# One transfer for a set of query or key rows, with the token order restored later, in a bucketed-attention and maxout kernel

## The chip, the cores and the metric

The kernel runs on one core of one Trainium2 chip. The metric is the device time of one execution in microseconds (us); the median of several runs is compared. Five engines work side by side, each on its own queue of instructions and in order: TensorE (PE; PEld is its weight load), VectorE (DVE), ScalarE (ACT), GpSimd (POOL) and SyncE (SP), which here only issues transfers. ACT and POOL issue transfers too.

## The reference

Four batches of eight heads with 768 tokens of 64 features. Each token gets six hash bits from a projection; a query may attend only to keys with the same bits. The output rows, heads side by side, go through a maxout layer of three matrices and an output matrix.

```
q_bits = (einsum('bhsd,dk->bhsk', q, proj) > 0)          # k = 6 bits, likewise k_bits
mask = q_bucket[:, :, :, None] == k_bucket[:, :, None, :]
scores = where(mask, (1 / sqrt(D)) * q @ k.T, -1e9)
attn = softmax(scores)                                   # + 1e-9 in the denominator
x = (attn @ v).transpose(0, 2, 1, 3).reshape(B * S, H * D)     # 3072 x 512
h = maximum(maximum(x @ w1, x @ w2), x @ w3)             # d_ff = 768
out = h @ w_out                                          # 3072 x 512, fp32
```

## The kernel before

**Scores and bits in one matmul.** For each head a tile `S` holds, over the partitions, the 64 features of the keys or queries in bf16 and, below them, the bits as plus or minus a half. One matmul over 70 or 72 partitions thus gives the scaled score plus a term that is largest where all bits agree, and the exponential with a bias (line 304) makes everything else vanish. No maximum is taken. The sums of the weights and the weighted values are matmuls of their own (`sums`, line 351, and `values`, line 373), four heads side by side in four groups of 32 columns.

**Units.** The work is cut into 192 units, 48 for each batch: one unit is the scores of three blocks of 128 keys with 256 queries (batch 0) or of two blocks with 384 queries (later batches), and one exponential over 768 columns into a tile `AT`. `scores(u + 1)` is issued at the head of unit u; two score tiles `sc` in PSUM go round, so scores(u) wait for exponential u - 2. Nine chunks (`chunks`: three of 256 queries for batch 0, two of 384 for each other batch) end with a burst for each half of the heads (`burst`): sums, reciprocals, then values for even and odd features, written normalised to `xT`. The maxout layer of a finished chunk (`ffn_groups`) is spread over the units that follow, about one group for each. Batch 0 takes heads 0 and 1 of its three chunks first, then 2 and 3, then 4 to 7.

**The order is written by hand.** `when(u, f)` puts a piece of work into unit u, behind the scores of the next unit; pieces of one unit go in the order in which they were put. Nothing is reordered later: each engine runs its instructions in this order.

**Four banks.** Everything on PE besides the scores writes to one of four PSUM banks, `ms`. `bank()` takes the one that was given back first, `give` returns it. The list goes round at build time, so the n-th taker waits until the taker four places ahead of it has been read out by DVE or ACT.

**How queries and keys get in.** The eight heads of batch 0 come in pairs, 0 to 3: `load_pair` (SP, the first also ACT), PE transposes (`pair_turn`, line 122), DVE or ACT copies to fp32 tiles `T32` (`pair_keep`, 131 and 129), POOL scales and narrows into `S` (`pair_place`, 136), and PE hashes (`pair_hash`, 149, for pairs 2 and 3; `head_hash`, 169, for the first two), DVE tests the bits (152, 174) and, for pairs 2 and 3, SP sends them into `S` (158). Pair 2 is the third pair: its transposes are put at units 6, 7, 9 and 10, its hash at unit 12; pair 3's transposes at 11, 13, 14 and 15, its hash at 18. Pair 2 is first read at unit 24, pair 3 at unit 28.

All other batches come as sets of four heads, keys and queries apart (side 1 and 0; g = 2 to 7, two for each batch): `load_quad` (194) puts the rows of four heads on 4 x 32 partitions; `turn` (200) transposes 32 x 32 blocks on DVE in four instructions for a set; `narrow` (205) scales and narrows on POOL in two; `place` (210) has SP send the four heads into `S`; `quad_hash` (219, 222) hashes and tests a set pair and SP sends the bits (230). `hash_at`, `SPREAD` and `need` give the units.

**Rows and tokens.** Block m of 128 keys holds, at partition or column p, token 6p + m (values are loaded so, line 238, and the output rows are written so, `block_of` and `rows`). In `load_quad` partition t of a head holds, for cc = 0 to 3, the six tokens from 192 cc + 6t on, so a row comes in four runs of 1536 bytes, and `turn` then leaves the columns in the order (m, cc, t), which is (m, p).

**Issuers.** Per unit, POOL's queue holds the placing and narrowing, the values' and weights' loads (`load_v`, `load_weights`, which also narrow while they transfer), the sets' loads (for g = 4 to 7 one head for each of four units, from 14 units ahead of the first `turn` on; the queries of g = 2 at unit 13), and a memset that makes finished `AT` tiles fit the later batches (388). SP holds the bits, the placings, the keys of g = 2 (at the very start), both sides of g = 3 (units 23 and 27) and the output.

**The end.** After the last unit come three groups of the maxout layer of chunk 7, the last burst (chunk 8, heads 4 to 7), the rest of chunk 7 and the whole layer of chunk 8. Its last 128 output rows are written in two halves of 256 columns (`last`, 431): the first is copied out and sent by ACT (435, 439), the second by DVE (437) and SP.

Of the kernel before, what the change touches and what calls it, by code (L numbers as in the profile page):

```python
# [17 lines left out]
def kernel(  # L18
# [12 lines left out]
    nc = tc.nc  # L31
# [62 lines left out]
    def give(i):  # L94
        free_banks.append(i)
# [91 lines left out]
    def load_quad(side, g, xs, eng):  # L187
        if (side, g) not in nat:
            start_set((side, g), [(side, 4 * g + x) for x in range(4)])
        for x in xs:  # L190
            b, h = divmod(4 * g + x, H)
            src = (q, k)[side][b, h].rearrange("(cc t m) d -> t cc (m d)", cc=CC, t=Q)
            dst = nat[side, g][x * Q : (x + 1) * Q, :].rearrange("t (cc w) -> t cc w", cc=CC)
            eng.dma_start(dst, src)  # L194
# [7 lines left out]
    def narrow(name, u):  # L202
        if name not in t16:
            t16[name] = t16_pool.tile([P, 2, S], BF16, tag="T16", name="T16")
        nc.gpsimd.tensor_scalar(out=t16[name][:, u, :], in0=t32[name][:, u, :], scalar1=RS, scalar2=1.0,  # L205
# [6 lines left out]
    def quad_hash(g):  # L212
        i, bp = bank()
        ts = [t32.pop((side, g)) for side in range(2)]
        for u in range(2):
            for side in range(2):
                for j in range(2):
# [4 lines left out]
        nc.vector.tensor_scalar(out=bits[:], in0=bp[:, 0:HALF], scalar1=0.0, scalar2=0.5,  # L222
                                op0=AluOp.is_gt, op1=AluOp.subtract)
# [115 lines left out]
    def burst(c, i):  # L339
# [3 lines left out]

        def sums(m0, m1):
            if m0 == 0:
                held["s"] = bank()
# [17 lines left out]
        def values(side, m0, m1):  # L364
            if m0 == 0:
                held[side] = bank()
# [28 lines left out]
    def ffn_groups(c):  # L395
# [31 lines left out]
        def last(part, tb):  # L427
            k_, ps = bank()
            cs = slice(part * DM // 2, (part + 1) * DM // 2)
            for fb in range(NFB):  # L430
                nc.tensor.matmul(ps[:, 0 : DM // 2], hts[fb][:, tb * P : (tb + 1) * P], wout_sb[:, fb, cs],
                                 start=(fb == 0), stop=(fb == NFB - 1))
            osb = out_rows(tb)
            if part == 0:
                nc.scalar.copy(osb[:, cs], ps[:, 0 : DM // 2])
            else:
                nc.vector.tensor_copy(osb[:, cs], ps[:, 0 : DM // 2])
            give(k_)
            (nc.scalar, nc.sync)[part].dma_start(rows[block_of(b, q0 // P + tb)][:, cs], osb[:, cs])

        def item(tb, part):
            def go2(part, tb=tb):
                if c == NCH - 1 and tb == w // P - 1:
                    last(part, tb)
# [30 lines left out]
    with tc.manual_schedule():  # L475
# [10 lines left out]
        load_quad(1, 2, range(4), nc.sync)  # L486
# [9 lines left out]
        load_weights(0)  # L496
# [28 lines left out]
        scores(1)  # L525
        pair_turn(0, 1, 1, bk)
# [30 lines left out]
        when(12, pair_hash, 2)  # L557
        when(13, t32.pop, 2)
# [5 lines left out]
        when(13, load_quad, 0, 2, range(4), nc.gpsimd)  # L564
        for u, side, g in ((23, 1, 3), (27, 0, 3)):
            when(u, load_quad, side, g, range(4), nc.sync)
# [96 lines left out]
```

## Time and profile before

| | us |
|---|---|
| median of 3 runs | 266.45 |
| lowest and highest | 266.21, 267.57 |
| the profiled execution | 266.3 |
| its span, first to last instruction | 264.2 |
| granted TensorE clock | 1.0 of full speed |

| DMA queue (issued by) | packets | MB | share of 16 engines |
|---|---|---|---|
| q0 (POOL) | 8128 | 13.37 | 26.8% |
| q1 (SP) | 12048 | 16.66 | 21.9% |
| q10 (ACT) | 512 | 0.53 | 0.6% |

The page of a profile gives the busy time of each engine, the chain of work that ended last (followed back from the last instruction), and groups of instructions with their line, engine, operation, written and read tiles and shapes, their number, the busy time, the mean time of one, and behind a second bar the idle time of the engine just before them with what ended it. In the timeline a row has the start, the length, the engine, the line and the shape of a run of instructions, and in brackets the idle time ahead of it. An engine's name with a q is its queue, where transfers are issued. Matmuls are pipelined: the length of one is longer than the step from one to the next, so starts are compared rather than lengths.

### The profile page before, as it was taken

The numbers are of one execution on the slowest core, as the hardware profiler recorded it, in microseconds if no ns is written. First come the engines' busy times: TensorE is split into PE (matmuls) and PEld (weight loads), VectorE is DVE, ScalarE is ACT, GpSimd is POOL, SyncE is SP. The second block draws the span as 40 slices with busy tenths as digits, with TensorE's granted clock in tenths as the row PEclk, the third lists the DMA queues.
The fourth block names the chain that finished last, engine by engine and source line by source line (L and its number), as shares of the span: only waits on it lengthen the run. The fifth ranks groups of instructions, "written<-read, shape, count | busy, mean of one in ns | idle before, by whom it ended". The sixth has DMA issues, their size and how long they took to land.

```text
span 264.2 us, 6478 instructions
## 1 busy us (share of the span) xinstructions
PE 257.7 (98%) x2503; PEld 154.1 (58%) x2503; DVE 208.6 (79%) x493; ACT 177.5 (67%) x257; POOL 70.1 (27%) x132
## 2 busy tenths in 40 slices
PE   8999999999999999999999999999999999999995
PEld 3655557866766666565555555555555555554552
DVE  2897676977699999978999997999759795887361
ACT  3696785676958684965869589484886859581322
POOL 5577752355042536230141612011000000000000
PEclk9999999999999999999999999999999999999999
DMA  6998899959822863980063662802030003000303
GB/s 197 308 236 168 171 238 228 220 100 203 215 85 63 184 172 47 269 195 23 0 198 102 98 142 48 205 4 62 15 122 1 0 2 120 2 0 2 119 0 119
DMA packets 20717, 30.95 MB, mean 117 GB/s; under 512 B 2608, under 2 KB 15248, under 8 KB 20688
## 3 DMA queue, kind: packets, MB, share of 16 engines
q0 software_dynamic: 8128, 13.37, 26.8%
q1 hardware_dynamic: 12048, 16.66, 21.9%
q10 hardware_dynamic: 512, 0.53, 0.6%
q8 instruction: 19, 0.31, 0.5%
q14 instruction: 10, 0.08, 0.1%
HBM read 25.17 MB, written 6.29 MB: 119 GB/s over the span
## 4 chain that ended last, share of the span: by engine, by line
PE 87%; DVE 6%; issue 2%; ACT 1%; DMA 1%; POOL 1%; ACTq 0%; DVEq 0%
PE ms L406 33%; PE sc L296 22%; PE ms L373 11%; PE ms L450 11%; PE ms L219 3%; PE ms L351 3%; PE ms L122 2%; DVE ht L415 2%; DVE ad L327 1%; ACT AT L304 1%; DMA nat<-in_q_dram 1%; DVE S L174 1%; PE ms L169 1%; PE ms L149 1%; POOL S L136 1%
## 5 line engine op out<-in xcount | busy, mean ns | idle before, releaser
L304 ACT ACTIVATE AT<-sc 128x768 f16<-128x768 f32 x192 | 152.4, 817 | 60.2 <-PE sc L296 56.8
L406 PE MATMUL ms<-xT,w_sb 128*128 128x384 f16 (+1 forms) x648 | 114.8, 307 | 0.1
L296 PE MATMUL sc<-S 72*128 72x384 bf16 (+1 forms) x432 | 93.6, 308 | 1.3 <-DVE S L174 0.5
L406 PEld LDWEIGHTS <-w_sb 128*128 128x128 f16 x648 | 62.7, 97 | 36.0 <-issue 0.4
L415 DVE TENSOR_TENSOR ht<-ht,ms 128x384 f16<-128x384 f16 (+1 forms) x108 | 54.3, 504 | 22.1 <-PE ms L406 11.3
L296 PEld LDWEIGHTS <-S 72*128 72x128 bf16 (+1 forms) x432 | 39.5, 98 | 33.2 <-issue 13.5
L205 POOL TENSOR_SCALAR T<-T 128x768 bf16<-128x768 f32 x24 | 22.9, 954 | 91.1 <-issue 47.5
L450 PE MATMUL ms<-wout_sb,ht 128*128 128x512 f16 x138 | 35.5, 378 | 0.0
L373 PE MATMUL ms<-AT,vo 128*32 128x385 f16 (+3 forms) x864 | 35.2, 309 | 0.3 <-DVE ht L415 0.3
L327 DVE TENSOR_TENSOR ad<-ad,AT 128x768 f16<-128x768 f16 x48 | 26.6, 554 | 2.1 <-ACT AT L304 1.3
L373 PEld LDWEIGHTS <-vo 128*32 128x32 f16 x864 | 22.6, 96 | 9.6 <-issue 1.8
L200 DVE STREAM_TRANSPOSE T<-nat 128x384 f32<-128x384 f32 x48 | 26.9, 565 | 0.0
L327 DVE TENSOR_TENSOR ad<-AT,AT 128x768 f16<-128x768 f16 x48 | 26.2, 546 | 0.2 <-ACT AT L304 0.2
L411 ACT CAST ht<-ms 128x384 f16<-128x384 f32 x36 | 17.3, 479 | 8.1 <-PE ms L406 8.1
L380 DVE SCALAR_TENSOR_TENSOR xT<-ms,sv,rb 128x384 f16<-128x384 f32 (+1 forms) x36 | 19.8, 567 | 1.4
L450 PEld LDWEIGHTS <-ht 128*128 128x128 f16 x138 | 13.3, 97 | 13.0 <-issue 0.3
L454 ACT COPY osb<-ms 128x512 f32<-128x512 f32 x21 | 12.3, 586 | 7.8 <-PE ms L450 6.3
L330 DVE TENSOR_TENSOR ad<-ad 128x384 f16<-128x384 f16 x32 | 15.5, 484 | 1.1
L136 POOL TENSOR_SCALAR S<-T 64x384 bf16<-64x384 f32 (+1 forms) x23 | 14.2, 619 | 6.3 <-DVE T L131 4.9
L358 DVE STREAM_TRANSPOSE ys<-ms 128x384 f32<-128x384 f32 (+1 forms) x18 | 9.6, 535 | 6.4 <-PE ms L351 6.2
L194 POOL DMA_DIRECT2D nat<-in_q_dram x20 | 11.1, 561 | 0.1
L174 DVE TENSOR_SCALAR S<-ms 6x384 bf16<-6x384 f32 x16 | 8.9, 554 | 2.2 <-PE ms L169 1.8
(48 smaller groups left out, 121.4 us busy)
## 6 DMA issues: line engine op xcount, KB each, us to landing
out_dram<-osb SPq DMA_DIRECT2D x21, 256.0 KB
S<-T SPq DMA_DIRECT2D x48, 96.0 KB
nat<-in_q_dram POOLq DMA_DIRECT2D x20, 192.0 KB, 6.3
vo<-in_v_dram POOLq DMA_DIRECT2D x8, 384.0 KB, 5.9
nat<-in_k_dram POOLq DMA_DIRECT2D x16, 192.0 KB, 5.5
w_sb<-in_moe_w_dram POOLq DMA_DIRECT2D x3, 768.0 KB, 8.6
nat<-in_k_dram SPq DMA_DIRECT2D x10, 192.0 KB
nat<-in_k_dram SPq DMA_DIRECT2D x3, 384.0 KB
```

The source lines that it names most:

```text
L136: nc.gpsimd.tensor_scalar(out=o, in0=i_, scalar1=RS, scalar2=1.0, op0=AluOp.mult, op1=AluOp.mult)
L200: nc.vector.transpose(t32[name][:, u, half * HALF : (half + 1) * HALF], i_)
L205: nc.gpsimd.tensor_scalar(out=t16[name][:, u, :], in0=t32[name][:, u, :], scalar1=RS, scalar2=1.0, op0=AluOp.mult, op1=AluOp.mult)
L296: nc.tensor.matmul(views[j], s_of[kn][0 : D + bits, kx, m * P : (m + 1) * P], s_of[qn][0 : D + bits, qx, q0 : q0 + w], start=True, stop=True)
L304: nc.scalar.activation(t[:, :, 0:w], whole, ActFn.Exp, bias=-SCALE * 0.25 * bits, scale=SCALE)
L327: nc.vector.tensor_tensor(out=sum_of[c, h][:], in0=t[0], in1=t[n], op=AluOp.add)
L373: nc.tensor.matmul(av[Q * x : Q * (x + 1), 0:n], v_at[2 * b + i][:, x, cb * D + side : (cb + 1) * D : 2], weights_of(c, 4 * i + x, m)[:, 0 ...
L380: nc.vector.scalar_tensor_tensor(out=xt_of(c)[:, 2 * i + side, 0:w], in0=av[:, 0:w], scalar=sv_of[b, i, side][:], in1=rb[0][:, 0:w], op0=A ...
L406: nc.tensor.matmul(ps[:, 0:w], w_sb[wi][:, jc, fb * P : (fb + 1) * P], xt[:, jc, 0:w], start=(jc == 0), stop=(jc == NJC - 1))
L411: nc.scalar.copy(hts[fb][:, 0:w], ps[:, 0:w])
L415: nc.vector.tensor_tensor(out=hts[fb][:, 0:w], in0=hts[fb][:, 0:w], in1=ps[:, 0:w], op=AluOp.max)
L450: nc.tensor.matmul(ps[:, 0:DM], hts[fb][:, tb * P : (tb + 1) * P], wout_sb[:, fb, :], start=(fb == 0), stop=(fb == NFB - 1))
```

## The change

1. `load_quad` fetches a set of four heads by one transfer: partition t of a head holds the 24 tokens from 24t on, one run of 6144 bytes. All sets are loaded so; those that came head by head (g = 4 to 7) are now put 13 units ahead of their first `turn`.
2. `turn` is unchanged, but a column of its output at (m, j, t), with j the former cc, now stands for token 24t + 6j + m, so position p = 4t + j. `narrow` and the bits' test of `quad_hash` put this in order: they read in sequence and write with a step of four elements (t), in rows of 32.
3. The hash of pair 2 moves from unit 12 to 14, behind pair 3's transposes of units 13 and 14.
4. In the last burst (chunk 8, heads 4 to 7) the sums and the even values take a score tile each instead of a bank (`own_bank`).
5. The last 128 x 512 outputs go in pieces of 256 (DVE, SP), 128 (ACT, ACT) and 128 columns (DVE, SP).
6. The first weight is loaded behind `scores(1)` instead of ahead of the first matmul.

```diff
     def give(i):
-        free_banks.append(i)
+        if i is not None:
+            free_banks.append(i)
...
-    def load_quad(side, g, xs, eng):
-        if (side, g) not in nat:
-            start_set((side, g), [(side, 4 * g + x) for x in range(4)])
-        for x in xs:
-            b, h = divmod(4 * g + x, H)
-            src = (q, k)[side][b, h].rearrange("(cc t m) d -> t cc (m d)", cc=CC, t=Q)
-            dst = nat[side, g][x * Q : (x + 1) * Q, :].rearrange("t (cc w) -> t cc w", cc=CC)
-            eng.dma_start(dst, src)
+    def load_quad(side, g, eng):
+        start_set((side, g), [(side, 4 * g + x) for x in range(4)])
+        b, h = divmod(4 * g, H)
+        eng.dma_start(nat[side, g][:], (q, k)[side][b, h : h + 4].rearrange("h (t m) d -> (h t) (m d)", t=Q))
...
-        nc.gpsimd.tensor_scalar(out=t16[name][:, u, :], in0=t32[name][:, u, :], scalar1=RS, scalar2=1.0,
+        o = t16[name][:, u, :].rearrange("p (m t j) -> p m j t", t=Q, j=CC)
+        i_ = t32[name][:, u, :].rearrange("p (m j t) -> p m j t", t=Q, j=CC)
+        nc.gpsimd.tensor_scalar(out=o, in0=i_, scalar1=RS, scalar2=1.0,
                                 op0=AluOp.mult, op1=AluOp.mult)
...
-        nc.vector.tensor_scalar(out=bits[:], in0=bp[:, 0:HALF], scalar1=0.0, scalar2=0.5,
-                                op0=AluOp.is_gt, op1=AluOp.subtract)
+        nc.vector.tensor_scalar(out=bits.rearrange("p (m t j) -> p m j t", t=Q, j=CC),
+                                in0=bp[:, 0:HALF].rearrange("p (m j t) -> p m j t", t=Q, j=CC),
+                                scalar1=0.0, scalar2=0.5, op0=AluOp.is_gt, op1=AluOp.subtract)
...
+        def own_bank(key):
+            if c == NCH - 1 and i == 1 and key != 1:
+                return None, sc_ps.tile([P, 2, 512], FP32, tag="sc", name="sc")[:, 0, :]
+            return bank()
+
         def sums(m0, m1):
             if m0 == 0:
-                held["s"] = bank()
+                held["s"] = own_bank("s")
...
         def values(side, m0, m1):
             if m0 == 0:
-                held[side] = bank()
+                held[side] = own_bank(side)
...
-        def last(part, tb):
+        def last(tb, cs, use_act):
             k_, ps = bank()
-            cs = slice(part * DM // 2, (part + 1) * DM // 2)
+            n = cs.stop - cs.start
             for fb in range(NFB):
-                nc.tensor.matmul(ps[:, 0 : DM // 2], hts[fb][:, tb * P : (tb + 1) * P], wout_sb[:, fb, cs],
+                nc.tensor.matmul(ps[:, 0:n], hts[fb][:, tb * P : (tb + 1) * P], wout_sb[:, fb, cs],
                                  start=(fb == 0), stop=(fb == NFB - 1))
             osb = out_rows(tb)
-            if part == 0:
-                nc.scalar.copy(osb[:, cs], ps[:, 0 : DM // 2])
+            if use_act:
+                nc.scalar.copy(osb[:, cs], ps[:, 0:n])
             else:
-                nc.vector.tensor_copy(osb[:, cs], ps[:, 0 : DM // 2])
+                nc.vector.tensor_copy(osb[:, cs], ps[:, 0:n])
             give(k_)
-            (nc.scalar, nc.sync)[part].dma_start(rows[block_of(b, q0 // P + tb)][:, cs], osb[:, cs])
+            (nc.scalar if use_act else nc.sync).dma_start(rows[block_of(b, q0 // P + tb)][:, cs], osb[:, cs])
...
                 if c == NCH - 1 and tb == w // P - 1:
-                    last(part, tb)
+                    if part == 0:
+                        last(tb, slice(0, DM // 2), False)
+                    else:
+                        last(tb, slice(DM // 2, 3 * DM // 4), True)
+                        last(tb, slice(3 * DM // 4, DM), False)
                     return
...
-        load_weights(0)
...
         scores(0)
         scores(1)
+        load_weights(0)
...
-        when(12, pair_hash, 2)
-        when(13, t32.pop, 2)
+        when(14, pair_hash, 2)
+        when(15, t32.pop, 2)
...
-        when(13, load_quad, 0, 2, range(4), nc.gpsimd)
+        when(13, load_quad, 0, 2, nc.gpsimd)
         for u, side, g in ((23, 1, 3), (27, 0, 3)):
-            when(u, load_quad, side, g, range(4), nc.sync)
+            when(u, load_quad, side, g, nc.sync)
...
-                    for x in range(4):
-                        when(us[0] - 14 + x, load_quad, side, g, (x,), nc.gpsimd)
+                    when(us[0] - 13, load_quad, side, g, nc.gpsimd)
```

More of the change, by code (lines that the diff above doesn't have):

```diff
@@ L485 @@
         load_pair(3, nc.sync)
[L486 removed]
+        load_quad(1, 2, nc.sync)
         nc.vector.memset(pj2[:], 0.0)
```

## The prediction

> **What bounds the kernel now.** I read the page's totals and its chain of waits first, then busy times by stage, then the timeline wherever TensorE (PE) is not gapless.
>
> ```profile
> span 264.2 us, 6478 instructions
> PE 257.7 (98%) x2503; PEld 154.1 (58%) x2503; DVE 208.6 (79%) x493; ACT 177.5 (67%) x257; POOL 70.1 (27%) x132
> PE 87%; DVE 6%; issue 2%; ACT 1%; DMA 1%; POOL 1%; ACTq 0%; DVEq 0%
> ...
> 84.00:236.00 152.00, 152.00 (x1344) 86.53 (x1342) 131.43 (x287) 110.02 (x164) 28.46 (x38) 1.00 0.37 90
> ```
>
> The last row is a stage: its length, then the busy time of PE, PEld, DVE, ACT and POOL (instructions in brackets), granted clock, DMA share and GB/s. From 84 to 236 us PE has no idle time at full clock: there, an edit that leaves the matmuls alone can only lose. GpSimd (POOL) and the transfers are 1% each of the chain. So the edits to the loads work on engines that set nothing, and what can be won lies before 84 us, behind 236 us and behind the last matmul.
>
> A busy PE can still be waiting in the middle of a group, so I compared the time that one kind of group takes at two places. This is the timeline around the hash of pair 2, and of pair 3 with its last two rows of PE; the very last row is ACT's exponentials grouped over 16 to 34 us.
>
> ```profile
> 17.46 2.99 ACT L304 ACTIVATE AT<-sc 128x768 f16<-128x768 f32 x4 [0.36 <-PE sc L296]
> 17.62 2.26 DVE L174 TENSOR_SCALAR S<-ms 6x384 bf16<-6x384 f32 x4
> ...
> 19.07 0.49 PE L296 MATMUL sc<-S 70*128 70x256 bf16 x3
> ...
> 19.90 1.49 DVE L131 COPY T<-ms 128x384 f32<-128x384 f32 x3
> 19.93 1.89 PE L149 MATMUL ms<-T,pj 128*32 128x384 f32 x8 [0.36 <-DVE S L174]
> ...
> 21.75 0.50 PE L296 MATMUL sc<-S 70*128 70x256 bf16 x3
> 22.08 0.49 PE L122 MATMUL ms<-iden,nat 128*128 128x128 f32 x3
> 22.28 2.92 ACT L304 ACTIVATE AT<-sc 128x768 f16<-128x768 f32 x4 [1.83 <-PE sc L296]
> ...
> 23.14 0.49 PE L296 MATMUL sc<-S 70*128 70x256 bf16 x3
> ...
> 26.69 0.85 PE L149 MATMUL ms<-T,pj 128*32 128x384 f32 x8
> 27.48 0.83 PE L296 MATMUL sc<-S 70*128 70x256 bf16 x6
> ...
> L304 ACT ACTIVATE AT<-sc 128x768 f16<-128x768 f32 x19 | 14.5, 811 | 4.3 <-PE sc L296 4.2
> ```
>
> The eight hash matmuls of pair 2 at 19.93 take 1.82 us up to the next scores at 21.75; those of pair 3 take 0.79 us, 26.69 to 27.48. The first eight come too early: their bank is held until the bits of line 174 are done (17.62 + 2.26 = 19.88), and they read what VectorE (DVE) is still copying out (three copies, 19.90 to 21.39, of which the first two are theirs). ACT then stands still for 1.83 us. And of ACT's 4.3 idle us in 16 to 34 us, 4.2 are waits for scores: PE's order sets the pace there, so time taken out of PE's queue is not eaten by ACT at once.
>
> **The change part by part.**
>
> *The hash, from unit 12 to 14.* In the new order scores(14), pair 3's transposes of unit 13, scores(15) and those of unit 14 go ahead of the hash. Three scores, or three transposes, take 0.33 us of PE (21.75 to 22.08). Scores(13) leave PE at 19.07 + 0.33 = 19.40. Scores(14) need the score tile of exponential 12: the row of 17.46 holds exponentials 10 to 13, ending at 20.45, the third near 19.7. So scores(14) at 19.75; transposes at 20.08 (their bank is free from 19.88); scores(15) behind exponential 13 at 20.47; transposes at 20.80; the hash at 21.15 (DVE's first two copies, its operands and its bank, are done near 20.9); and with 0.85 us for it scores(16) near 22.0 instead of 23.14: **-1.1 us**. Bounds: 0, if what follows waits for something else; at most 1.82 - 0.79, and 0.53 for PE's idle stretch from 19.40 to 19.93, so 1.56. The bits themselves come some 0.7 us later, as DVE then has two more copies ahead of them; they are read from unit 24 on, ten units behind the hash, and SP has nothing else queued that PE needs sooner.
>
> *The last burst's banks.* The sums and the first half of the values of the last chunk take score tiles instead of banks.
>
> ```profile
> 238.58 1.46 PE L450 MATMUL ms<-wout_sb,ht 128*128 128x512 f16 x6
> ...
> 239.39 1.21 DVE L415 TENSOR_TENSOR ht<-ht,ms 128x384 f16<-128x384 f16 x2
> ...
> 239.99 0.35 PE L351 MATMUL ms<-ad,ones 128*32 128x384 f16 x4
> ...
> 240.65 2.13 PE L373 MATMUL ms<-AT,vo 128*32 128x384 f16 x48 [0.31 <-DVE ht L415]
> ...
> 242.28 1.17 DVE L380 SCALAR_TENSOR_TENSOR xT<-ms,sv,rb 128x384 f16<-128x384 f32 x2
> ...
> 242.72 2.76 PE L450 MATMUL ms<-wout_sb,ht 128*128 128x512 f16 x12
> ```
>
> The values start at 240.65, right behind DVE's two maxima (239.39 + 1.21 = 240.60), which give back their bank. Line 450 needs (2.76 - 1.46) / 6 = 0.217 a matmul, so its six let go of PE at 239.88. The sums could follow there, and the values as soon as the four sums, side by side, have streamed, 0.16 us (half of the group of three scores, whose columns are twice as many), at 240.05: **-0.55 us**; at least the 0.31 that the row names, at most 0.6. Next to be late would be line 406, which reads the normalised rows, ready at 242.28 + 1.17 = 243.45; the twelve of line 450 ahead of it now last until 242.1 + 2.6 = 244.7 and still cover that.
>
> *The new end.* The last 512 columns go as 256 (DVE), 128 (ACT), 128 (DVE) instead of 256 (ACT), 256 (DVE).
>
> ```profile
> 259.61 1.47 PE L431 MATMUL ms<-wout_sb,ht 128*128 128x256 f16 x12
> ...
> 261.12 0.42 DVE L437 COPY nat<-ms 128x256 f32<-128x256 f32 x1 [3.27 <-PE ms L431]
> 261.57 0.33 SPq L439 DMA_DIRECT2D out_dram<-nat  x1
> ```
>
> Half of 0.217 for 512 columns is 0.11 for 256. Six matmuls of 256 become twelve of 128, at 0.055 (half again) to 0.11 (no gain, as each still loads 128 columns of weights): 0 to +0.65 us; I take a point nearer to the half, +0.2. DVE's last copy is half as wide, of 0.42 perhaps 0.1 is saved; the last transfer, issued at 261.57 and 2.6 us from the span's end, is half as large: 0 to 0.3, say 0.1. Together 0.0, from -0.4 to +0.6. The Trainium skill (TensorE: Matmul & The Clock Gate, Back-to-back issue gap) gives about 81 ns for a matmul of 128 columns with its weight load in a sustained stream; by it the twelve would cost +0.3 instead of +0.2. No run so far has that shape.
>
> *One transfer for a set, and what pays for it.* Rows of a line's instructions, of the transfers, and of the engines' groups:
>
> ```profile
> L194 POOL DMA_DIRECT2D nat<-in_q_dram x20: 553/553/608, 24.9 to 149.4; - x20
> nat<-in_q_dram POOLq DMA_DIRECT2D x20, 192.0 KB, 6.3
> nat<-in_k_dram POOLq DMA_DIRECT2D x16, 192.0 KB, 5.5
> L200 DVE STREAM_TRANSPOSE T<-nat 128x384 f32<-128x384 f32 x48 | 26.9, 565 | 0.0
> L205 POOL TENSOR_SCALAR T<-T x24: 826/981/1052, 33.2 to 178.5; 128x768 bf16<-128x768 f32 x24
> L222 DVE TENSOR_SCALAR bits<-ms x6: 549/558/558, 43.0 to 183.9; 128x384 bf16<-128x384 f32 x6
> L136 POOL TENSOR_SCALAR S<-T 64x768 bf16<-64x768 f32 x8 | 6.6, 827 | 2.7 <-DVE T L131 2.3
> L136 POOL TENSOR_SCALAR S<-T 64x384 bf16<-64x384 f32 x2 | 1.0, 508 | 0.2
> L539 POOL COPY pj<-pst 32x12 f32<-32x12 f32 x4 | 0.8, 199 | 0.2
> ```
>
> POOL issues 9 transfers instead of 36, 27 x 0.55 = 15 us less of its time; SP issues 3 instead of 12. DVE's transposes never sat idle ahead of them (0.0), so no load is late. A whole set now goes out two units ahead of the old last piece, and it takes some 6 us to land: 0. The price is that the narrowing and the bits' test write with a step of four elements. Line 136 gives GpSimd's law for outputs in sequence: (827 - 508) / 384 = 0.83 ns an element and 189 ns fixed, which makes 199 ns for 12 elements; line 539, whose output does have a step of four elements, takes 199. So I take the narrowing as unchanged; upper bound twice its 0.98 us. Even then it lies beside PE: POOL is busy for 28 of the 152 us after 84. The six tests could cost as much again, 0.56 each, on DVE, which has 20 us to spare in that stage: 0, at most +0.6 if one of them holds back a bank at each hash.
>
> *The first weight* goes to POOL behind the second scores. Two rows of the timeline and one of the weight tile:
>
> ```profile
> 4.84 0.71 POOL L246 DMA_DIRECT2D w_sb<-in_moe_w_dram  x1
> ...
> 9.81 6.37 POOL L136 TENSOR_SCALAR S<-T 64x384 bf16<-64x384 f32 x11 [2.60 <-DVE T L131]
> ...
> L406 PE MATMUL ms<-xT,w_sb x648: 269/324/328, 43.5 to 256.9; 128*128 128x384 f16 x108, 128*128 128x256 f16 x54
> ```
>
> The 2.60 us in which POOL waits for DVE before 9.81 hide its issue of 0.71; its first reader comes at 43.5. 0 either way; without that gap +0.7. The pairs' early loads have less beside them for 3 us, but no wait of PE or DVE behind 5 us is one for a load, so nothing is gained.
>
> **Sum:** -1.1 - 0.55 + 0.0 + 0 = -1.65 us. The profiled execution ran 266.3 us, 264.2 of span and 2.1 around it, so 264.65; it lies 0.15 below the median of 266.45, which makes **264.8 us**.
>
> **The rivals.**
>
> *B, the hash's gain is eaten.* PE may meet the next gate, a bank or ACT, two units later; then only the end remains: 266.45 - 0.55 = 265.9. For it: four banks go round at the pace of DVE's copies, and the three at 19.90 are a backlog. Against it: ACT waits for PE in the whole stage, and the two copies that the hash needs are done before PE would come to it.
>
> *C, slower: GpSimd's scattered output is slow.* The second batch's first set must lie in place at unit 48, whose scores are the third row here.
>
> ```profile
> 33.21 0.83 POOL L205 TENSOR_SCALAR T<-T 128x768 bf16<-128x768 f32 x1 [1.66 <-DVE T L200]
> ...
> 39.86 6.47 SPq L210 DMA_DIRECT2D S<-T  x8
> ...
> 55.62 0.49 PE L296 MATMUL sc<-S 72*128 72x384 bf16 x2
> ```
>
> Four narrowings of N us from 33.21 - 1.1 = 32.1 on, then the last four of eight placings (3.2), about as much for the bits' transfers, and 5.5 to land (an estimate, from the loads of POOL above) must fit before 55.62 - 1.1 = 54.5: N up to (54.5 - 32.1 - 11.9) / 4 = 2.6 us. From there on each us costs four; at N = 4 PE would stand for 5.5 us: 264.8 + 5.5 = 270.3. For it: 12 elements are a weak lever on the law above, and the new view runs through three free dimensions. Against it: it takes nearly three times today's time.
>
> **How the numbers follow.** 0.5% (1.3 us) is about what a measurement of this kernel can tell from no change: faster is below 265.1, slower above 267.8. My forecast gets 0.63, from 263.9 (hash 1.56, banks 0.6, end 0.4) to 265.6, of it 0.57 below 265.1. B gets 0.25, from 265.1 to 266.7, all within. C gets 0.12. So 0.57 faster, 0.31 the same, 0.12 slower, and a range from 263.9 to 266.7, which leaves C out.
>
> **What would show it.** Right: pair 2's eight hash matmuls reach the next scores in about 0.85 us, with scores(16) near 22.0; the last values follow their sums within 0.2 us; the narrowing stays between 0.83 and 1.1 us; PE still has no idle time from 84 to 236 us. Wrong: ACT or a bank holds PE between 22 and 40 us; line 205 above 2.6 us with PE idle before unit 48; 0.11 us a matmul in the 128-column pieces and a later end.

## The result, and the profile after

| | before | after |
|---|---|---|
| median of 4 runs each, same chip | 266.91 us | 275.0 us |
| lowest and highest | 266.21, 267.57 | 274.44, 275.46 |
| ratio, 95% interval | | 1.029 [1.025, 1.033] |

The forecast was 264.8 us with a range up to 266.7. The kernel came out 8.1 us slower than before instead of 1.65 us faster. From the page of the kernel after: the totals, the chain of waits, and two of its groups.

```profile
span 273.2 us, 6441 instructions
...
PE 260.1 (95%) x2509; PEld 155.0 (57%) x2509; DVE 224.7 (82%) x494; ACT 177.8 (65%) x257; POOL 81.1 (30%) x105
...
PE 64%; DVE 24%; issue 7%; ACT 2%; DMA 1%; POOL 1%; ACTq 0%; DVEq 0%
...
L204 POOL TENSOR_SCALAR T<-T 128x768 bf16<-128x768 f32 x24 | 49.1, 2046 | 94.2 <-DVE T L197 56.1
...
L330 DVE TENSOR_TENSOR ad<-ad 128x384 f16<-128x384 f16 x32 | 22.1, 689 | 1.1
```

VectorE's share of the chain went from 6% to 24% and its busy time from 208.6 to 224.7 us, although the change gives it hardly any work. GpSimd's narrowing (line 204, before 205) takes 2046 ns in the mean; before it took 954. The stage from 84 to 236 us, in which PE was busy for all 152.00 us before, now reads:

```profile
84.00:236.00 152.00, 146.26 (x1253) 82.64 (x1251) 136.65 (x274) 104.59 (x154) 36.01 (x24) 1.00 0.34 88
```

In the same 152 us there are 91 matmuls fewer; the clock is 1.00 in both. In the profiled executions the scores of unit 72 begin 1.0 us later than before (83.69 and 82.72), those of unit 120 5.8 us (148.82 and 143.06) and those of unit 168 9.5 us (216.04 and 206.52); behind that nothing more is lost (their spans are 9.0 us apart). The last narrowing ends at 189.3 us. PE's waits (who waited for whom: us in total, times, longest), first the only one listed before for VectorE behind 84 us, then those of the kernel after:

```profile
PE ms L373 <- DVE ht L415: 0.3, 1, 0.3
```

```profile
PE ms L356 <- DVE ad L330: 2.1, 2, 1.1
PE ms L411 <- DVE ht L420: 1.9, 5, 0.6
...
PE ms L411 <- DVE xT L385: 0.8, 2, 0.5
```

PE waits for VectorE, for line 330 (2.1 us) and line 420 (1.9). Line 330 adds two halves of an fp16 tile, both in SBUF, ahead of the matmuls of `sums`; the expectations below call these additions products. Its 32 instructions all have one shape. By line, first before, then after (ns: min/median/max):

```profile
L330 DVE TENSOR_TENSOR ad<-ad x32: 357/358/866, 121.9 to 239.1; 128x384 f16<-128x384 f16 x32
```

```profile
L330 DVE TENSOR_TENSOR ad<-ad x32: 357/358/1687, 126.5 to 248.6; 128x384 f16<-128x384 f16 x32
...
L204 POOL TENSOR_SCALAR T<-T x24: 1912/2061/2172, 32.9 to 187.2; 128x768 bf16<-128x768 f32 x24
L221 DVE TENSOR_SCALAR bits<-ms x6: 1000/1010/1028, 43.9 to 193.4; 128x384 bf16<-128x384 f32 x6
```

The median stays at 358 ns; the longest grows from 866 to 1687. In both kernels eight of the 32 are long, and these eight are just the ones that begin during a narrowing. The timeline shows which ones are long. The same place in the order of work, before and then after:

```profile
125.00 0.52 DVE L327 TENSOR_TENSOR ad<-ad,AT 128x768 f16<-128x768 f16 x1
...
125.22 0.98 POOL L205 TENSOR_SCALAR T<-T 128x768 bf16<-128x768 f32 x1 [10.25 <-issue]
...
125.55 0.86 DVE L330 TENSOR_TENSOR ad<-ad 128x384 f16<-128x384 f16 x1
```

```profile
126.55 0.36 DVE L330 TENSOR_TENSOR ad<-ad 128x384 f16<-128x384 f16 x1
...
129.38 0.52 DVE L327 TENSOR_TENSOR ad<-ad,AT 128x768 f16<-128x768 f16 x1
129.62 2.06 POOL L204 TENSOR_SCALAR T<-T 128x768 bf16<-128x768 f32 x1 [9.92 <-issue]
...
129.93 1.69 DVE L330 TENSOR_TENSOR ad<-ad 128x384 f16<-128x384 f16 x1
```

Before, GpSimd ends at 125.22 + 0.98 = 126.20 and the addition begun meanwhile at 125.55 + 0.86 = 126.41. After, GpSimd ends at 131.68 and the addition at 131.62; alone (126.55) it takes 0.36. So **an addition that begins during a narrowing is held until shortly before the narrowing's end** (taking 0.36 us for itself, until 0.15 us before it in the first case and 0.42 in the second), already before the change. The addition of line 327 at 129.38, begun ahead of the narrowing, takes its usual 0.52: the first to start is not disturbed. This is what the Trainium skill states (SBUF — State Buffer, Who interferes with whom): the port pair that VectorE shares with GpSimd is an exclusive lock for a whole instruction, and a VectorE instruction with two SBUF inputs has to wait for a GpSimd instruction that reads SBUF. The trace agrees, 0.36 against 1.69 us. How such a hold reaches PE, in the kernel after:

```profile
104.79 2.17 POOL L204 TENSOR_SCALAR T<-T 128x768 bf16<-128x768 f32 x1 [3.47 <-DVE T L197]
...
105.92 1.18 DVE L327 TENSOR_TENSOR ad<-AT,AT 128x768 f16<-128x768 f16 x1
107.03 0.41 DVE L420 TENSOR_TENSOR ht<-ht,ms 128x256 f16<-128x256 f16 x1
107.36 0.57 DVE L363 STREAM_TRANSPOSE ys<-ms 128x384 f32<-128x384 f32 x1
...
109.11 1.14 DVE L385 SCALAR_TENSOR_TENSOR xT<-ms,sv,rb 128x384 f16<-128x384 f32 x2
...
109.78 0.38 PE L411 MATMUL ms<-xT,w_sb 128*128 128x256 f16 x2 [0.48 <-DVE xT L385]
```

Line 327 lasts until 107.10; behind it in VectorE's order come the maximum that frees a bank, the burst's reciprocals and `xT`, and PE waits for `xT`. The rows with a PSUM operand (line 420, 0.41) are not held. Where VectorE's 16.1 us more went, by groups with mean ns, line 330 before and then the kernel after:

```profile
L330 DVE TENSOR_TENSOR ad<-ad 128x384 f16<-128x384 f16 x32 | 15.5, 484 | 1.1
```

```profile
L327 DVE TENSOR_TENSOR ad<-ad,AT 128x768 f16<-128x768 f16 x48 | 28.8, 600 | 2.1 <-ACT AT L304 1.3
L327 DVE TENSOR_TENSOR ad<-AT,AT 128x768 f16<-128x768 f16 x48 | 28.2, 588 | 0.2 <-ACT AT L304 0.2
L197 DVE STREAM_TRANSPOSE T<-nat 128x384 f32<-128x384 f32 x48 | 26.9, 564 | 0.0
...
L221 DVE TENSOR_SCALAR bits<-ms 128x384 bf16<-128x384 f32 x6 | 6.1, 1012 | 1.7 <-PE ms L218 1.0 <-DMA S<-T 0.4 <-issue 0.3
L365 DVE TENSOR_SCALAR rr<-ys 128x8 f32<-128x8 f32 x6 | 4.1, 687 | 0.2
```

Against before: line 330 +6.6 (15.5 to 22.1), line 327 +4.2, the tiny `rr` of the bursts +3.1 (172 to 687 ns; both its operands lie in SBUF), and the six bits' tests +2.8, which are not held but slower themselves (555 to 1012 ns). Lying in SBUF with all operands is not enough to be held: nine of line 197's transposes, from SBUF to SBUF, begin during a narrowing (0.3 us or more before its end) and take 0.57 us at most, and their mean is 564 ns where it was 565.

The hash, the last burst and the end show in the timeline of the kernel after:

```profile
22.05 0.85 PE L150 MATMUL ms<-T,pj 128*32 128x384 f32 x8
22.83 0.50 PE L296 MATMUL sc<-S 70*128 70x256 bf16 x3
...
248.10 1.46 PE L459 MATMUL ms<-wout_sb,ht 128*128 128x512 f16 x6
...
249.49 0.35 PE L356 MATMUL sc<-ad,ones 128*32 128x384 f16 x4
249.67 1.15 PE L378 MATMUL sc<-AT,vo 128*32 128x384 f16 x24
...
251.72 2.76 PE L459 MATMUL ms<-wout_sb,ht 128*128 128x512 f16 x12
...
266.02 2.75 PE L459 MATMUL ms<-wout_sb,ht 128*128 128x512 f16 x12
...
268.61 1.49 PE L436 MATMUL ms<-wout_sb,ht 128*128 128x256 f16 x18
...
270.21 0.29 DVE L442 COPY nat<-ms 128x128 f32<-128x128 f32 x1 [0.31 <-PE ms L436]
```

Hash to scores 0.78 us (1.82 before), and scores(16) at 22.83 where 22.0 was forecast: the first scores of this execution begin at 8.38 us, 0.76 later than before (7.62); values 0.18 behind their sums, and from the six of line 459 to its twelve 3.62 us (4.14 before); from the last twelve to the span's end 273.2 - 266.02 = 7.18 (7.19 before).

### The profile page after: what moved, and what is told of

Its sections match the earlier page's. It is cut to its first block, busy times and chain, and to the rows that moved or that the text cites. A ratio compares the mean times of both kernels' runs of the same rounds, so it can differ in the third digit from the quotient of the medians.

```text
span 273.2 us, 6441 instructions
## 1 busy us (share of the span) xinstructions
PE 260.1 (95%) x2509; PEld 155.0 (57%) x2509; DVE 224.7 (82%) x494; ACT 177.8 (65%) x257; POOL 81.1 (30%) x105
## 4 chain that ended last, share of the span: by engine, by line
PE 64%; DVE 24%; issue 7%; ACT 2%; DMA 1%; POOL 1%; ACTq 0%; DVEq 0%
PE ms L411 24%; PE sc L296 16%; PE ms L459 9%; PE ms L378 8%; DVE ad L327 6%; DVE ht L420 6%; DVE T L197 2%; PE ms L356 2%; ACT AT L304 2%; PE ms L218 2%; DVE xT L385 2%; DVE ad L330 1%; DMA nat<-in_q_dram 1%; PE ms L123 1%; DVE S L175 1%
## 5 line engine op out<-in xcount | busy, mean ns | idle before, releaser
L204 POOL TENSOR_SCALAR T<-T 128x768 bf16<-128x768 f32 x24 | 49.1, 2046 | 94.2 <-DVE T L197 56.1
L378 PE MATMUL ms<-AT,vo 128*32 128x385 f16 (+3 forms) x840 | 34.5, 308 | 0.5 <-DVE ht L420 0.3
L327 DVE TENSOR_TENSOR ad<-ad,AT 128x768 f16<-128x768 f16 x48 | 28.8, 600 | 2.1 <-ACT AT L304 1.3
L378 PEld LDWEIGHTS <-vo 128*32 128x32 f16 x864 | 23.3, 96 | 11.9 <-issue 5.0
L327 DVE TENSOR_TENSOR ad<-AT,AT 128x768 f16<-128x768 f16 x48 | 28.2, 588 | 0.2 <-ACT AT L304 0.2
L330 DVE TENSOR_TENSOR ad<-ad 128x384 f16<-128x384 f16 x32 | 22.1, 689 | 1.1
L385 DVE SCALAR_TENSOR_TENSOR xT<-ms,sv,rb 128x384 f16<-128x384 f32 (+1 forms) x35 | 19.2, 565 | 1.3
L363 DVE STREAM_TRANSPOSE ys<-ms 128x384 f32<-128x384 f32 (+1 forms) x17 | 9.0, 531 | 3.0 <-PE ms L356 2.9
L367 DVE STREAM_TRANSPOSE rb<-rr 128x384 f32<-128x384 f32 (+1 forms) x18 | 9.6, 534 | 0.6
```

Source lines behind the costliest of these rows:

```text
L204: nc.gpsimd.tensor_scalar(out=o, in0=i_, scalar1=RS, scalar2=1.0, op0=AluOp.mult, op1=AluOp.mult)
L327: nc.vector.tensor_tensor(out=sum_of[c, h][:], in0=t[0], in1=t[n], op=AluOp.add)
L330: nc.vector.tensor_tensor(out=t[:, 0, :], in0=t[:, 0, :], in1=t[:, 1, :], op=AluOp.add)
L378: nc.tensor.matmul(av[Q * x : Q * (x + 1), 0:n], v_at[2 * b + i][:, x, cb * D + side : (cb + 1) * D : 2], weights_of(c, 4 * i + x, m)[:, 0 ...
L385: nc.vector.scalar_tensor_tensor(out=xt_of(c)[:, 2 * i + side, 0:w], in0=av[:, 0:w], scalar=sv_of[b, i, side][:], in1=rb[0][:, 0:w], op0=A ...
```

## The experiments

Theory P: VectorE's instructions with all operands in SBUF stand for as long as one GpSimd instruction runs, so the price is the length of the narrowing. (As the transposes show, this names too many instructions; the additions and `rr` are the ones meant.) Rival S: writing with a step hurts by itself. Rival T: GpSimd's total counts. Rival N: the narrowing delivers the rows too late. Theories B and L of the first four runs blame the bits' test and the single transfer. All ratios are against the kernel before on the same chip. Its median was 266.61 to 266.91 us on the chips used, so times of rows from different chips compare to some 0.3 us.

| kernel | narrowing, mean ns | longest line 330, ns | us | ratio |
|---|---|---|---|---|
| after | 2046 | 1687 | 275.0 | 1.029 [1.025, 1.033] |
| after, narrowing in sequence | 954 | 868 | 266.92 | 1.000 [0.998, 1.002] |
| after, bits' test in sequence | 2047 | 1687 | 273.35 | 1.025 [1.022, 1.028] |
| before, narrowing scattered | 2047 | 1693 | 274.78 | 1.031 [1.028, 1.035] |
| the other edits only | 954 | 866 | 265.44 | 0.996 [0.994, 0.998] |
| before, two inputs in sequence | 1595 | 1511 | 271.99 | 1.019 [1.018, 1.021] |
| before, narrowing twice | 973 and 888 | 866 | 267.01 | 1.001 [1.000, 1.002] |
| after, narrowing in thirds | 857 | 542 | 268.8 | 1.009 [1.006, 1.011] |
| after, narrowing on ScalarE | 1925 (ScalarE) | 359 | 289.16 | 1.084 [1.081, 1.086] |
| after, reading with a step | 1669 | 1591 | 272.82 | 1.023 [1.022, 1.025] |
| after, one transfer only | 951 | 866 | 266.22 | 0.998 [0.996, 0.999] |
| other edits, halves | 635 | 547 | 265.75 | 0.997 [0.996, 0.999] |
| hash only | 952 | 868 | 265.47 | 0.996 [0.994, 0.997] |
| banks only | 951 | 866 | 266.39 | 0.999 [0.998, 1.000] |
| end only | 952 | 864 | 267.69 | 1.005 [1.003, 1.007] |
| hash and banks | 952 | 867 | 265.38 | 0.995 [0.992, 0.997] |

### Parts undone and parts alone

The narrowing of the kernel after in sequence:

```diff
-        o = t16[name][:, u, :].rearrange("p (m t j) -> p m j t", t=Q, j=CC)
-        i_ = t32[name][:, u, :].rearrange("p (m j t) -> p m j t", t=Q, j=CC)
-        nc.gpsimd.tensor_scalar(out=o, in0=i_, scalar1=RS, scalar2=1.0,
+        nc.gpsimd.tensor_scalar(out=t16[name][:, u, :], in0=t32[name][:, u, :], scalar1=RS, scalar2=1.0,
```

> The changed kernel with the narrowing reading and writing in sequence again (the bits' test still permutes, so keys and queries of batches 1 to 3 keep the transfer's order in S). Theory P (the scattered narrowing holds GpSimd for 2.05 us instead of 0.95, and VectorE's instructions with all operands in SBUF stand still until it ends): 264.5 to 265.5 us, VectorE's busy time back from 224.7 to about 211. Theory B (the scattered bits' test on VectorE): 273 to 275. Theory L (one transfer for a set): 273 to 275.

Only the bits' test in sequence:

```diff
-        nc.vector.tensor_scalar(out=bits.rearrange("p (m t j) -> p m j t", t=Q, j=CC),
-                                in0=bp[:, 0:HALF].rearrange("p (m j t) -> p m j t", t=Q, j=CC),
-                                scalar1=0.0, scalar2=0.5, op0=AluOp.is_gt, op1=AluOp.subtract)
+        nc.vector.tensor_scalar(out=bits[:], in0=bp[:, 0:HALF], scalar1=0.0, scalar2=0.5,
+                                op0=AluOp.is_gt, op1=AluOp.subtract)
```

> The changed kernel with the bits' test writing in sequence again (the bits of batches 1 to 3 stand in the transfer's order). Theory P: 273.5 to 275, the test back at 0.56 us. Theory B: 265 to 267. Theory L: 273 to 275.

The kernel before with nothing but the scattered narrowing (the first diff the other way round):

> The kernel before with only the scattered narrowing put in (S of batches 1 to 3 is then out of order). Theory P: 275.5 to 277 us, that is the loss of the changed kernel without its gains of 1.65 us at the hash and the end. Theories B and L: 266 to 267.

The kernel before with hash, banks, end and first weight; loads, narrowing and bits' test as before:

> The kernel before with the hash at unit 14, the score tiles for the last sums and values, the new end and the later first weight, and with the old loads, narrowing and bits' test. If the prediction's steps for these hold: 264.4 to 265.2 us, the hash -1.1 and the banks -0.55, the end 0. If the later first weight costs the 0.75 us by which the changed kernel's first scores were late: 265.2 to 266.

The scattered narrowing alone costs 274.78 - 266.78 (the kernel before beside it) = 8.0 us, and undoing it alone gives 8.1 back. So neither the transfer nor the other edits carry the loss. The third kernel is 0.7 us below what P said, which had put the whole loss on the narrowing, with the other edits' gains on top. The bits' test in sequence gives 1.65 us by the medians (275.0 to 273.35), though the intervals of the two ratios overlap. The fourth kernel (265.44) lies above the 265.2 of the forecast steps, and in the range written for a later first weight that costs 0.75 us. The traces don't bear that out: the first scores begin at 7.33 to 8.15 us in the eight profiled executions with the weight first and at 7.44 to 8.38 in the nine with it later. The first kernel missed its expectation by 1.4 us at least. Its timeline has a store in the way:

```profile
140.61 0.59 ACT L461 COPY osb<-ms 128x512 f32<-128x512 f32 x1 [1.71 <-DMA out_dram<-osb]
...
142.34 0.48 PE L294 MATMUL sc<-S 72*128 72x384 bf16 x2 [1.25 <-ACT AT L302]
```

ScalarE stood 1.71 us for its output buffer, and PE for ScalarE. Whether the single transfer does that, or the longer bits' tests, was tried further down.

### Length, scatter, total

Before, with a GpSimd instruction of two inputs, all in sequence (`rs_t`, one value a partition, is filled once at the start):

```diff
-        nc.gpsimd.tensor_scalar(out=t16[name][:, u, :], in0=t32[name][:, u, :], scalar1=RS, scalar2=1.0,
-                                op0=AluOp.mult, op1=AluOp.mult)
+        nc.gpsimd.tensor_tensor(out=t16[name][:, u, :], in0=t32[name][:, u, :],
+                                in1=rs_t[:, 0:1].to_broadcast((P, S)), op=AluOp.mult)
```

> The kernel before, with GpSimd's narrowing as an instruction of two inputs (the second is one value a partition, repeated), in sequence: the same numbers, no step in what it reads or writes. It tells the length of the instruction from the scattered writing. Theory P (VectorE's instructions with all operands in SBUF stand for as long as GpSimd's instruction runs, whatever makes it long): the time goes with its length; at 0.83 to 1.0 us as before, 266 to 267.5; at 1.9 us or more, 273 to 276, with the longest products of line 330 as long as the instruction, less 0.2 us. Rival S (writing with a step is what hurts VectorE, by collisions in the memory): 266 to 267.5 whatever its length, and line 330 at 0.48 us in the mean.

```profile
127.46 1.64 POOL L206 TENSOR_TENSOR T<-T,rs_t 128x768 bf16<-128x768 f32 x1 [8.91 <-issue]
127.80 1.51 DVE L331 TENSOR_TENSOR ad<-ad 128x384 f16<-128x384 f16 x1
```

No step anywhere, and the addition still ends 0.21 us behind GpSimd (129.10 and 129.31), with 5.1 us lost. S falls. At 1595 ns the loss lies between the kernel before and the scattered one, as P says, though 1 us under the 273 written for 1.9 us and more.

The narrowing made twice, no instruction longer:

```diff
+        nc.gpsimd.tensor_scalar(out=t16[name][:, u, :], in0=t32[name][:, u, :], scalar1=RS, scalar2=1.0,
+                                op0=AluOp.mult, op1=AluOp.mult)
```

> The kernel before with each narrowing made twice, the second over the first, so that GpSimd's time doubles (22.9 to 46 us) and no instruction gets longer. Theory P in its plain form (a hold lasts for one instruction of GpSimd and VectorE comes in between two): line 330 from 0.48 to 0.55-0.62 us in the mean, its longest still under 1.05 us, 268 to 271. Rival T (the total of GpSimd's narrowing decides, however it is cut): longest products near 1.7 us and 274 to 275.5, as with the scattered narrowing. Rival S (writing with a step is what hurts): 266.5 to 267.5.

```profile
132.74 1.05 POOL L205 TENSOR_SCALAR T<-T 128x768 bf16<-128x768 f32 x1 [4.82 <-DVE T L200]
133.13 0.86 DVE L332 TENSOR_TENSOR ad<-ad 128x384 f16<-128x384 f16 x1
133.87 0.83 POOL L207 TENSOR_SCALAR T<-T 128x768 bf16<-128x768 f32 x1
133.92 1.19 DVE L329 TENSOR_TENSOR ad<-AT,AT 128x768 f16<-128x768 f16 x1
```

The addition of line 332 ends at 133.99, soon after the first of the two; the next one is held by the second, until 135.11. GpSimd works nearly as long as with the scattered narrowing (973 + 888 ns), so the rows come later too, yet the time is that of before. T falls, and N as the account of the 8 us: what counts is the length of one hold. I had expected 268 to 271 and 0.55 to 0.62 us for line 330 in the mean; it stayed at 0.48, and two short holds cost less than I took from P.

The scattered narrowing in thirds:

```diff
-        nc.gpsimd.tensor_scalar(out=o, in0=i_, scalar1=RS, scalar2=1.0,
-                                op0=AluOp.mult, op1=AluOp.mult)
+        for w in range(3):
+            nc.gpsimd.tensor_scalar(out=o[:, 2 * w : 2 * w + 2], in0=i_[:, 2 * w : 2 * w + 2], scalar1=RS,
+                                    scalar2=1.0, op0=AluOp.mult, op1=AluOp.mult)
```

> The kernel after with each scattered narrowing cut into three instructions of 256 elements, 0.65 to 0.8 us each by a third of 2.05 us and up to 0.1 us for the start of each. Theory P in its plain form: a product of line 330 stands for one third at most, its longest about 1.1 us (0.36 and 0.75), its mean near 0.5 us; 268 to 271. Rival T: 273.5 to 276, longest products 1.7 us or more, as the three follow each other without a gap for VectorE.

Same elements, same scatter, and 6.2 us come back: the longest addition is 542 ns, where P's 1.1 us was too long. The profiled execution is the slowest of the five (270.41 us). It has another wait, by PE's waits and then by its chain (start, us):

```profile
PE sc L297 <- DMA S<-bits: 1.7, 1, 1.7
```

```profile
61.38 9.13 DMA S<-bits
```

PE stands for it at 71.03, at unit 60, the first to read heads 4 to 7 of the second batch. Unit 48, where the prediction's rival C puts its wait, begins at 54.94 us and doesn't wait for its set. Nor is the length of the thirds shown to be the cause: the kernel after issues the same bits at the same 61.38 us, and its unit 60 begins at 70.02 without that wait. Why they took 9.13 us to land here, and what makes up the 1.9 us that the median still loses, stays open.

The scattered narrowing on ScalarE:

```diff
-        nc.gpsimd.tensor_scalar(out=o, in0=i_, scalar1=RS, scalar2=1.0,
-                                op0=AluOp.mult, op1=AluOp.mult)
+        nc.scalar.mul(o, i_, RS)
```

> The kernel after with the scattered narrowing on ScalarE and none on GpSimd after the first pairs. Theory P: with GpSimd out of the way the products of line 330 are back at 0.36 us, VectorE's busy time falls from 225 us to 203-207, ScalarE's grows by 24 instructions of 0.8 to 2 us, and the time is 264 to 267. Rival N (the loss is that the narrowing, twice as long, delivers the rows too late, and VectorE's long products are a side effect): with a narrowing of 1.5 us or more on ScalarE behind its exponentials the time stays at 273 or above.

```profile
PE sc L295 <- ACT AT L303: 14.8, 14, 1.5
```

All 32 additions are back at 357 to 359 ns, as P says, but its time was wrong by 22 us: 24 instructions of 1925 ns stand ahead of exponentials in ScalarE's queue, and PE waits 14.8 us for those. That is N's number without N's reason.

The narrowing of the kernel after in the order of its output, so that it reads with a step of 128 bytes:

```diff
-        o = t16[name][:, u, :].rearrange("p (m t j) -> p m j t", t=Q, j=CC)
-        i_ = t32[name][:, u, :].rearrange("p (m j t) -> p m j t", t=Q, j=CC)
+        o = t16[name][:, u, :].rearrange("p (m t j) -> p m t j", t=Q, j=CC)
+        i_ = t32[name][:, u, :].rearrange("p (m j t) -> p m t j", t=Q, j=CC)
```

> The kernel after with the same narrowing and the same result, but the instruction goes through its elements in the order of the output: it writes in sequence and reads with a step of 32 elements (128 bytes). Theory P (the length of one instruction of GpSimd is what holds VectorE) has the time follow the length: 0.85 to 1.0 us gives 266 to 267.5, 1.6 us gives 270 to 272 as in the run with two inputs, 2 us or more gives 273.5 to 276. Rival S (a step in writing hurts by itself): 266 to 268 whatever the length.

1669 ns and 272.82 us: again by length, 0.8 us above the 272 written for 1.6 us. Loss over lengthening, per narrowing: 5.1 us for 0.64 us (two inputs), 5.9 for 0.72 (reading with a step, against 266.92), 8.0 for 1.09 (scattered), so **7.3 to 8.2 us for each us by which the 24 narrowings grow**, whatever makes them grow.

### What is left: transfer, halves, hash, banks, end

The kernel after with narrowing and bits' test both in sequence (the first two diffs together):

> The kernel after with the narrowing and the bits' test both in sequence, so that of the part for the loads only the one transfer is left (the rows' order is then not that of the reference). Theory B (the rest that the kernel after with the narrowing in sequence lost against the hash, banks, end and first weight alone, 266.9 to 265.4, is the bits' test, 0.45 us more of VectorE six times): 265.2 to 265.7. Rival L (the single transfer of 768 KB holds a store of outputs up, and ScalarE stands for the store's buffer): 266.3 to 267, with ScalarE's copy to the output waiting for the store for 2 us or more.

The median of 266.22 lies between the two theories. Its profile, of the fastest of twelve executions (264.76 us), does not have the long wait of the first kernel; at the same copy it shows

```profile
138.33 0.59 ACT L460 COPY osb<-ms 128x512 f32<-128x512 f32 x1 [0.54 <-DMA out_dram<-osb]
```

So a fast execution goes without the wait; whether the slower ones have it, this profile can't tell. The interval of the ratio meets those of the hash alone and of the other edits without the transfer. The median is 0.8 us above that of the other edits; taken as independent, the two intervals leave room from a gain of 0.2 us to a cost of 1.3 (an estimate). No gain shows, and what the single transfer costs stays open. Without the long narrowing the bits' test, too, is worth only 0.7 us (266.92 to 266.22), within the intervals.

The other edits, with the narrowing (in sequence) in halves:

```diff
+        for w in range(2):
+            cs = slice(w * HALF, (w + 1) * HALF)
+            nc.gpsimd.tensor_scalar(out=t16[name][:, u, cs], in0=t32[name][:, u, cs], scalar1=RS, scalar2=1.0,
+                                    op0=AluOp.mult, op1=AluOp.mult)
```

> The kernel before with the hash at 14, the last burst's banks, the new end and the later first weight, and with the narrowing (in sequence) cut into two halves of 384 elements, 0.5 to 0.6 us each. Theory P: line 330 from 0.48 us to 0.40-0.44 in the mean, its longest near 0.6 us instead of 0.87. Whether that shows in the time: 264.6 to 265.4 if the wait of the matmuls for VectorE after 104 us was real, 265.4 (as without the cut) if PE had no gap there to give back; slower than 266 only if GpSimd's longer total is late for the placing of rows.

The holds shrink (longest 547 ns) and the time does not (265.75 against 265.44): holds of the length that the kernel before had cost nothing that shows. By these runs the price begins above it.

The hash alone:

```diff
-        when(12, pair_hash, 2)
-        when(13, t32.pop, 2)
+        when(14, pair_hash, 2)
+        when(15, t32.pop, 2)
```

> The kernel before with the third pair's hash at 14 instead of 12 and nothing else. By the traces (first scores to first sums 16.64 us before, 15.55 us in each kernel with the hash at 14) the time falls by 1.1 us: 265.5 to 266.0. Rival (the matmuls' gain is given back later, as VectorE or ScalarE become late): 266.4 to 266.9. With the hash, banks, end and weight together at 265.4, the rest is then worth 0.2 to 0.5 us.

266.61 - 265.47 = 1.14 us, as forecast.

The last burst's banks alone (with `own_bank` and `give` as in the change):

```diff
-                held["s"] = bank()
+                held["s"] = own_bank("s")
...
-                held[side] = bank()
+                held[side] = own_bank(side)
```

> The kernel before with the last burst's banks alone. The prediction's step says -0.55 us (0.31 to 0.6): 266.0 to 266.4 against about 266.7 for the kernel before, and the stretch from line 450's six matmuls to its twelve after the last burst at 3.6 us instead of 4.14. Rival (the stage is shortened and the time given back behind it, or the freed waits were no longer than the clock's spread): 266.6 to 266.9.

```profile
239.43 1.46 PE L456 MATMUL ms<-wout_sb,ht 128*128 128x512 f16 x6
...
243.04 1.25 PE L456 MATMUL ms<-wout_sb,ht 128*128 128x512 f16 x5
```

The second row shows five of the twelve, those up to the end of the view. The stretch is 3.61 us, as predicted, and the median falls by 0.29; the interval reaches from a gain of 0.7 us to none.

The new end alone (with `last` as in the change):

```diff
-                    last(part, tb)
+                    if part == 0:
+                        last(tb, slice(0, DM // 2), False)
+                    else:
+                        last(tb, slice(DM // 2, 3 * DM // 4), True)
+                        last(tb, slice(3 * DM // 4, DM), False)
```

> The kernel before with the new end alone (the last 512 columns in 256, 128 and 128). The prediction's step says 0.0 (-0.4 to +0.6): 266.5 to 266.9. Rival (the fourth copy and the smaller stores cost some 0.4 us, as two profiles with it end 0.44 us later): 267.0 to 267.3, with 7.6 us from line 460's last twelve matmuls to the span's end instead of 7.2.

```profile
257.88 2.75 PE L454 MATMUL ms<-wout_sb,ht 128*128 128x512 f16 x12
...
262.07 0.29 DVE L437 COPY nat<-ms 128x128 f32<-128x128 f32 x1 [0.31 <-PE ms L431]
```

1.0 us slower, more than either side expected. The span is 265.5 us, so from the last twelve to the end it is 7.62 us here, and 7.18 in the kernel after, although copies and issues stand alike: VectorE's last copy ends 4.48 us behind the start of the twelve in both. The 0.44 us come behind it, in each profile that has the new end and the old loads, and in none of the kernels with the new loads. What makes them, and the other half microsecond, no run isolates. Beside the hash and the banks the end's price doesn't show: all four edits together take 265.44 us.

Hash and banks, with the old end:

> The kernel before with the hash at 14 and the last burst's banks, the old end, the old loads. If the banks' step is real and the end costs nothing: 265.0 to 265.3, 0.3 to 0.5 us under the hash alone (265.47). If the end costs 0.4 us: also 265.0, and below all four together (265.44). If the banks give nothing: 265.4 to 265.6.

265.38 us, between the ranges written for it: with the hash alone (265.47) the fastest version; the two can't be told apart, and both beat the kernel before by about 0.5%.

## Why the prediction was wrong

**The step that failed** is the narrowing: "So I take the narrowing as unchanged; upper bound twice its 0.98 us. Even then it lies beside PE: POOL is busy for 28 of the 152 us after 84." The length came out at its upper bound (2.05 us). It did lie beside PE, but not beside VectorE, and a share of busy time says nothing about whom an instruction shuts out while it runs. What the runs showed in its place: an addition of VectorE that begins during a narrowing stands nearly to its end, and PE waits for VectorE. This term, taken as 0, is +8.0 us alone on the kernel before, and the hold was already to be read there: line 330, of one single shape, had 358 ns in the median, 866 at most and 484 in the mean, so (484 - 358) / (866 - 358) = a quarter of its 32 additions were held.

- **The law for the narrowing** rested on twelve elements of line 539. At (2046 - 189) / 768 = 2.4 ns an element instead of 0.83, twelve differ by 19 ns: the row could not tell.
- **"DVE has 20 us to spare"**: true as a sum, wrong where it matters. The held additions stand between a chunk's scores and its burst, with PE's next bank or `xT` behind them.
- **The bits' test** went from 0.56 to 1.01 us, near its upper bound of twice; undone in the kernel after it gives 1.65 us by the medians, not at most 0.6.
- **The hash**: forecast -1.1, measured -1.14 alone. Rival B is out.
- **The banks**: -0.52 us in the stage, where -0.55 was forecast; -0.29 in the median, not told from zero.
- **The end**: 0.0 in the kernel after, as forecast, but in part by luck. The 128-column matmuls cost half as much as the 256-column ones, 18 matmuls in 1.49 us against 12 in 1.47 before: +0.02 instead of +0.2. The narrower copy gave its 0.1. The smaller transfer gave nothing: from the last copy's end to the span's end it is 2.70 us, 2.66 before. By the rows, the Trainium skill's 81 ns for a 128-column matmul (cited in the prediction, with +0.3 for the twelve) does not hold here. Alone the end lost 1.0 us.
- **Transfer and first weight**: nothing gained that shows, as forecast; what the transfer costs is open, and the first weight was not run alone.
- **Rival C** had the right side, slower because of the scattered output, with the wrong mechanism: unit 48 begins at 55.55 us in the kernel after and at 55.62 before, so no set was late for it.

Sum of the runs' parts: the other edits together 265.44 - 266.78 = -1.34, the narrowing +8.0, the bits' test +1.65, so +8.3 us; measured +8.1. That it fits so well is partly luck: the transfer is not in it, the test's 1.65 holds only beside the long narrowing, and the end alone would add 1.0.

## What to carry to other kernels

An engine that is idle for most of a stage can still shut another one out while it runs; look for groups of one shape whose longest instruction is far above the median, and see what ran beside those. Where GpSimd works beside additions of VectorE with both inputs in SBUF, the length of one GpSimd instruction is a price of its own: keep it short, or cut it, as long as the sum still arrives in time. Here the new layout of the loads won nothing that shows, and the instructions that put the order right with a step paid for it.

## What the hardware showed unexpectedly

- Writing bf16 with a step of four elements takes 1.91 us at least on GpSimd for 128 x 768, against 0.83 in sequence; reading fp32 with a step of 32 elements 1.54; a second, repeated input 1.46. On ScalarE the scattered writing takes 1.90 us and more, and VectorE's test from PSUM 1.01 instead of 0.56.
- GpSimd's narrowing varies too, 826 ns at least and 1052 at most before; the one shown at 125.22, begun during an addition of line 327, took 0.98 us. The trace of the kernel before shows that it is held too: the eight narrowings that begin with no addition of line 327 running take 826 to 833 ns, the sixteen that begin during one 977 to 1052.
- A hold lasts for one instruction: between two narrowings back to back (at 132.74 and 133.87), the waiting addition gets in.
